# A mixture-of-experts layer behind sigmoid attention: the second expert product in row form, and the gathered rows turned by VectorE through DRAM

## The chip, the core and the metric

The kernel runs on one core of a Trainium2 chip. Its time is the device time of one execution in microseconds (us); lower is better. A core has five engines that work side by side, each on its own in-order list of instructions: TensorE (PE in the profile, with its weight loads shown apart as PEld), VectorE (DVE), ScalarE (ACT), GpSimd (POOL) and SyncE (SP, which here only issues DMAs). Matmul results go to PSUM, which has eight banks of 512 fp32 words per partition; a tile of two banks is called wide below.

## The reference: what is computed

```python
scores = scale * np.matmul(q, k.transpose(0, 1, 3, 2)) - np.log(S)   # 8 x 12 heads, 448 tokens, 64 dims
attn = 1.0 / (1.0 + np.exp(-scores))
x = np.matmul(attn, v)            # brought to 3584 tokens x 768
logits = x @ w_gate               # 3584 x 8
order = np.argsort(-logits.flatten())
for idx in order:                 # greedy: each expert takes at most 448 tokens
    tok, e = idx // 8, idx % 8
    if assigned[tok] < 0 and counts[e] < 448:
        assigned[tok] = e; counts[e] += 1
for e in range(8):                # x: 768 -> 1024 -> 768
    out[assigned == e] = np.maximum(x[assigned == e] @ w1[e], 0) @ w2[e]
```

Every expert ends with exactly 448 tokens.

## The kernel before, in words

**Attention (first 278 us or so).** For every pair of heads TensorE makes scores, ScalarE the sigmoid, TensorE the product with v. The result is kept turned, and `rows` writes it as rows of 768 to the DRAM tensor `xs`.

**Routing.** The greedy assignment is done expert by expert by the class `Router`. One phase finds the next expert that fills up, and the threshold that its 448th token has, by a search of 16 steps (`search`, L157 to L218), then makes the list of its tokens (`pick`, `place`, `lists`; the list is `idx`, L293). From the second phase on a search step is VectorE work alone: three counting passes (L173), two small block transposes (L189, L195), a sum and some scalar operations. TensorE takes part at the ends of a phase: L162 turns the keys, L224 turns the threshold `kap` that the search has found (VectorE L217), L252, L257, L258, L284 and L291 make the list. Phase 0 runs before the experts, phases 1 to 7 while the experts run.

**Experts.** `moe(kx)` (L660) makes the two products of one expert. Every fp32 operand is split into a high part and a rest (`wh`/`wl`, `xh`/`xl`, `hh`/`hl`), and a product is the sum of three matmuls (high-high, high-rest, rest-high). Both products hold the weights still (128 x 128) and move the 448 tokens: 144 matmuls of 448 columns for the first product (L680 to L684), 144 for the second (L715 to L719). Because of that the second product comes out turned, 768 features by 448 tokens; `untranspose` (L641) brings it back, in 12 pairs of TensorE transposes per expert (L645), each with a copy by ScalarE (L650), and then scatters the rows to `out` (L653). The weights come in pieces through SP's queue (`load_w`, L573) and are split by ScalarE (L596) and GpSimd (L598; for the last two experts every other one on VectorE).

**Rows of the next expert.** When the list of the next expert is there, `prepare` (L752) puts its work into `chores`: four gathers of 128 rows from `xs` (L618, GpSimd's queue), and eight `xturn` (L621), each three TensorE transposes (L632), a ScalarE copy (L635) and a VectorE subtraction (L636) that yield `xh` and `xl`, the turned input of the first product.

**What sets the order.** Nothing is scheduled at run time: the order of each engine's list is written by the loop at the end (L767 to L787). It walks through the matmuls of `moe`, adds an assumed price for each to `clock` (MM, 189 ns), and, when the clock passes a due time, puts in the next step of the router (due times from T_DVE and the like) or the next chore. So the search steps of phase k+1 stand in VectorE's list among the chores for the expert of phase k, and L224 stands in TensorE's list after as many matmuls as the assumed prices make of a search.

**PSUM.** `ps_t` has two single banks (transposes), `ps_s` two wide tiles (the products), `ps_a` two single banks (the router).

## Time and profile before

| | us |
|---|---|
| three runs, median | 890.27 (887.0, 890.27, 893.16) |
| the profiled execution, its own time | 887.23 |
| its span, from the first to the last instruction | 885.5 |
| first matmul of the experts (L680) | 335.31 |
| start of the last matmul of the experts (L719) | 877.14 |

| engine | busy, us | share of the span |
|---|---|---|
| PE | 837.8 | 95% |
| PEld | 639.0 | 72% |
| DVE | 531.4 | 60% |
| POOL | 467.4 | 53% |
| ACT | 456.2 | 52% |

How to read it: shares over the whole span mix the attention with the experts. For the experts, from 335 us on, the views that count are the busy time by stretch, the instructions in order of time on one engine (with the idle time ahead of each and who ended it), and the groups of instructions with their mean duration. A matmul's shown duration contains its way through the array and overlaps its neighbours, so its cost in a row of matmuls is the distance from one start to the next.

### The profile page before, as it was taken

Reading aid. Unit: us, or ns where it says so; the run is one execution under the profiler, and the core shown is the slowest. Engines: PE = TensorE matmul, PEld = TensorE weight load, DVE = VectorE, ACT = ScalarE, POOL = GpSimd, SP = SyncE. Lnnn points to the kernel's source line nnn. Section 1 sums busy time; section 2 is a strip of 40 time slices with the busy share of each in tenths; the row PEclk is TensorE's granted clock in tenths of the full one; section 3 lists DMA queues with packets and bytes.
Section 4 is the critical chain, followed back from the end, with each engine's and each line's share of the span. In section 5 each row is a group of like instructions: output and inputs, shape, how many; then the busy total and the mean of one; then the engine's idle time right before and its main releaser. Section 6 shows DMA issues by size and latency. Waiting matters only on the chain.

```text
span 885.5 us, 16232 instructions
## 1 busy us (share of the span) xinstructions
PE 837.8 (95%) x5507; PEld 639.0 (72%) x5507; DVE 531.4 (60%) x2047; ACT 456.2 (52%) x610; POOL 467.4 (53%) x449
## 2 busy tenths in 40 slices
PE   6999999999998729998999999999999999999996
PEld 3455455455555518987988988988888888889996
DVE  4665555555554778958869779779689521421110
ACT  6777777777774724434424424434434434443431
POOL 9645444444400014846864964873883882752651
PEclk9999999999999969999999999999999999999999
DMA  9876666665603945434443542452552542632511
GB/s 172 168 144 127 132 125 123 131 126 120 138 12 100 299 161 153 136 107 161 136 133 117 146 156 75 157 164 95 153 164 70 178 146 72 228 111 72 192 49 63
DMA packets 203507, 117.57 MB, mean 133 GB/s; under 512 B 143936, under 2 KB 193088, under 8 KB 203424
## 3 DMA queue, kind: packets, MB, share of 16 engines
q1 hardware_dynamic: 190688, 83.03, 36.0%
q0 software_dynamic: 10880, 33.28, 11.9%
q8 instruction: 43, 0.70, 0.3%
q10 hardware_dynamic: 1856, 0.23, 0.2%
q14 instruction: 40, 0.33, 0.1%
HBM read 94.47 MB, written 22.02 MB: 132 GB/s over the span
## 4 chain that ended last, share of the span: by engine, by line
PE 77%; DVE 8%; DMA 5%; issue 4%; POOL 3%; ACT 1%; SPq 1%; POOLq 0%; ACTq 0%; DVEq 0%
PE tp L461 13%; PE sc L437 11%; PE sc L682 8%; PE sc L680 8%; PE sc L684 8%; PE sc L717 6%; PE sc L719 6%; PE sc L715 6%; PE tp L467 2%; DMA xs<-xr 2%; DVE r_junk L173 2%; PE sc L447 2%; PE tp L645 2%; DMA xr<-xs,r_idx 2%; PE tp L632 2%
## 5 line engine op out<-in xcount | busy, mean ns | idle before, releaser
L598 POOL TENSOR_TENSOR wl<-wr,wh 128x768 fp32r<-128x768 f32 (+1 forms) x96 | 205.9, 2155 | 134.6 <-ACT wh L596 126.9
L427 ACT ACTIVATE at<-sc,bias 128x896 f32<-128x896 f32 x168 | 161.0, 1006 | 63.1 <-PE sc L447 38.2
L372 POOL DMA_DIRECT2D nkq<-in_q_dram x188 | 118.6, 646 | 111.5 <-DVE kqT L412 104.7
L719 PE MATMUL sc<-hh,wl 128*128 128x448 f32 (+2 forms) x400 | 151.4, 378 | 0.0
L717 PE MATMUL sc<-hl,wh 128*128 128x448 f32 (+2 forms) x400 | 145.4, 364 | 0.1
L684 PE MATMUL sc<-xh,wl 128*128 128x448 f32 (+2 forms) x396 | 145.4, 367 | 0.0
L682 PE MATMUL sc<-xl,wh 128*128 128x448 f32 (+2 forms) x396 | 144.9, 366 | 0.0
L715 PE MATMUL sc<-hh,wh 128*128 128x448 f32 (+2 forms) x400 | 143.9, 360 | 0.0
L680 PE MATMUL sc<-xh,wh 128*128 128x448 f32 (+2 forms) x396 | 143.8, 363 | 0.0
L173 DVE TENSOR_SCALAR_CACHE_REDUCE r_junk<-r_KE,r_T 128x224 bf16<-128x224 f32 x315 | 123.2, 441 | 0.1
L461 PE MATMUL tp<-at,nv 128*64 128x448 f32 x576 | 118.8, 548 | 0.0
L596 ACT ACTIVATE wh<-wr 128x768 fp32r<-128x768 f32 (+1 forms) x112 | 102.0, 939 | 13.2 <-DMA wr<-in_moe_w_dram 13.1
L692 POOL TENSOR_TENSOR hl<-yt,hh 128x896 fp32r<-128x896 f32 x32 | 68.3, 2136 | 44.5 <-ACT yt L691 41.8
L421 DVE TENSOR_TENSOR kqL<-kqT,kqH 128x896 fp32r<-128x896 f32 (+1 forms) x49 | 52.6, 1073 | 58.3 <-ACT kqH L419 58.2
L688 ACT ACTIVATE hh<-sc 128x896 fp32r<-128x896 f32 x32 | 29.5, 920 | 111.0 <-PE sc L684 111.0
L618 POOL DMA_INDIRECT xr<-xs,r_idx x32 | 32.0, 1002 | 97.5 <-ACT wh L596 86.7
L717 PEld LDWEIGHTS sc<-hl,wh 128*128 128x128 f32 x400 | 75.2, 188 | 7.0 <-issue 1.1
L598 DVE TENSOR_TENSOR wl<-wr,wh 128x768 fp32r<-128x768 f32 (+1 forms) x16 | 25.1, 1571 | 91.7 <-ACT wh L596 91.5
L461 PEld LDWEIGHTS tp<-at,nv 128*64 128x64 f32 x576 | 37.1, 136 | 59.1 <-issue 57.9
L682 PEld LDWEIGHTS sc<-xl,wh 128*128 128x128 f32 x396 | 74.5, 188 | 6.3 <-issue 0.5
L715 PEld LDWEIGHTS sc<-hh,wh 128*128 128x128 f32 x400 | 75.6, 189 | 4.4
L680 PEld LDWEIGHTS sc<-xh,wh 128*128 128x128 f32 x396 | 74.7, 189 | 5.5
(156 smaller groups left out, 1323.7 us busy)
## 6 DMA issues: line engine op xcount, KB each, us to landing
wr<-in_moe_w_dram SPq DMA_DIRECT2D x64, 384.0 KB
wr<-in_moe_w_dram SPq DMA_DIRECT2D x48, 512.0 KB
xs<-xr SPq DMA_DIRECT2D x32, 336.0 KB
nkq<-in_k_dram SPq DMA_DIRECT2D x190, 56.0 KB
nkq<-in_q_dram POOLq DMA_DIRECT2D x188, 56.0 KB, 2.6
nv<-in_v_dram SPq DMA_DIRECT2D x92, 96.0 KB
nr<-in_v_dram SPq DMA_DIRECT2D x46, 32.0 KB
xr<-xs,r_idx POOLq DMA_INDIRECT x32, 4.4
```

Source lines behind the costliest of these rows:

```text
L173: nc.vector.tensor_scalar(junk, KE, T[:, i:i + 1].bitcast(F32), None, OP.is_ge, OP.add, accum_out=cnt[:, i:i + 1])
L372: qn.dma_start(t[o:o + 32, n], rws[x])
L427: nc.scalar.activation(a, p[:, :, :S], AF.Sigmoid, bias=bias, scale=1 / math.sqrt(D))
L461: nc.tensor.matmul(p[j * 64:j * 64 + 64, :S], nat["v", b, g][:, h0 + j, c, :], AT[b, pr, c][:, j, :], start=(c == 0), stop=(c == 2 and pr ...
L596: nc.scalar.activation(hi, raw[u], AF.Copy)
L598: eng.tensor_tensor(lo, raw[u], hi.bitcast(F32), OP.subtract)
L680: nc.tensor.matmul(ph[:, f, lo:hi], wh[:, a, fs], xh[:, dd, lo:hi], start=st, stop=False)
L682: nc.tensor.matmul(ph[:, f, lo:hi], wh[:, a, fs], xl[:, dd, lo:hi], start=False, stop=False)
L684: nc.tensor.matmul(ph[:, f, lo:hi], wl[:, a, fs], xh[:, dd, lo:hi], start=False, stop=en)
L715: nc.tensor.matmul(py[:, d2, :w], wh[:, a, dsl], h1, start=st, stop=False)
L717: nc.tensor.matmul(py[:, d2, :w], wh[:, a, dsl], h2, start=False, stop=False)
L719: nc.tensor.matmul(py[:, d2, :w], wl[:, a, dsl], h1, start=False, stop=(j == 1 and a == 3))
```

## The change

It has four parts, and nothing in attention or in the routing itself changes.

1. **Second product in row form.** The hidden values are now held still, 128 tokens at a time, and 384 columns of `w2` move. The result comes out as rows of tokens and needs no turning back. 448 tokens are three blocks of 128 and one of 64; for the last one the high part and the rest of 64 tokens each share one block of 128 (`hr`), whose two halves are added afterwards (L748 to L753). Per expert 176 matmuls of 384 columns (L738) stand where 144 of 448 columns and 24 transposes stood. `w2` comes in eight pieces of 128 x 768, not six of 128 x 1024.
2. **Rows of the experts from the third on turned by VectorE.** `stage` writes the gathered rows to a DRAM buffer `xq` (SP's queue), `fetch` reads them back in four parts, so that 32 tokens by 192 features lie on each group of 32 partitions, and `vturn` turns them in blocks of 32 x 32 on VectorE (L641), copies on ScalarE (L643) and subtracts on VectorE (L644). Four `vturn` per expert stand where eight `xturn` stood. Feature 6p + a now stands on partition p, so `w1` is read in that order, and the remaining `xturn` (experts 0 and 1) take every sixth column.
3. **PSUM.** `ps_t` is gone, `ps_s` has three wide tiles, and `xturn` uses the router's banks.
4. **Prices and buffers.** MM2 = 164 ns for the 384-column matmuls, fewer row buffers, W_DVE moved so that it still names the last two experts.

The order of the instructions moves with it. VectorE, in the search of phase 4 before (the rows are those of expert 3; `xl` is the rest of the turned rows, `r_junk` the counting passes):

```order
L636 TENSOR_TENSOR xl<-tp,xh 128x3x128
L173 TENSOR_SCALAR r_junk,c_CN<-r_KE,r_T 128x224 x3
L189 STREAM_TRANSPOSE r_ct<-c_CN 128x32
L191 TENSOR_SCALAR rt<-c_kk,r_J 128x3
L193 TENSOR_REDUCE r_s_6891<-r_ct 128x2
L195 STREAM_TRANSPOSE r_ct<-r_s_6891 128x32
L197 TENSOR_SCALAR r_j_6887,r_acc<-r_ct 128x3
L210 SCALAR_TENSOR_TENSOR r_T<-r_acc,rt 128x3
L212 TENSOR_SCALAR r_J<-r_acc,r_J 128x1
L636 TENSOR_TENSOR xl<-tp,xh 128x3x128 x2
```

Now, in the search of phase 3 (the rows are those of expert 2):

```order
L641 STREAM_TRANSPOSE xt<-xw 128x256 x3
L644 TENSOR_TENSOR xl<-xt,xh 128x3x256
L173 TENSOR_SCALAR r_junk,c_CN<-r_KE,r_T 128x224 x3
L189 STREAM_TRANSPOSE r_ct<-c_CN 128x32
L191 TENSOR_SCALAR rt<-c_kk,r_J 128x3
L193 TENSOR_REDUCE r_s_6161<-r_ct 128x2
L195 STREAM_TRANSPOSE r_ct<-r_s_6161 128x32
L197 TENSOR_SCALAR r_j_6157,r_acc<-r_ct 128x3
L210 SCALAR_TENSOR_TENSOR r_T<-r_acc,rt 128x3
L212 TENSOR_SCALAR r_J<-r_acc,r_J 128x1
L641 STREAM_TRANSPOSE xt<-xw 128x256 x3
L644 TENSOR_TENSOR xl<-xt,xh 128x3x256
```

Where one subtraction stood between two search steps, three transposes and a subtraction of twice the width stand, with a ScalarE copy between them. There are four such groups per expert, and for the experts 2, 3, 4 and 5 they lie in the searches of phases 3, 4, 5 and 6; for the experts 6 and 7 they come after the last search.

TensorE, in a second product (`yt` is the turned result before; `hb` and `hr` are the hidden values now). Before:

```order
L645 MATMUL tp<-ident,yt 128x128 x2
L719 MATMUL sc<-hh,wl 128x448
L715 MATMUL sc<-hh,wh 128x448
L717 MATMUL sc<-hl,wh 128x448
L719 MATMUL sc<-hh,wl 128x448
```

Now, and no transpose stands among them:

```order
L738 MATMUL sc<-wh,hr 128x384
L738 MATMUL sc<-wl,hr 128x384
L738 MATMUL sc<-wh,hb 128x384 x2
L738 MATMUL sc<-wl,hb 128x384
L162 MATMUL rt<-ident,r_KT 128x112 x2
```

Counted over the whole list, 207, 212, 218 and 221 matmuls of the products stand between L162 and L224 in the phases 3 to 6 (74, 112, 152 and 176 of them of 384 columns, the others of 448); before it was 196 to 198 of 448 columns with 24 transposes of rows and 16 to 24 of results.

SP's queue, where the rows of expert 2 go to DRAM and back (`wr` are the weights); before, only the weights stood there:

```order
L584 DMA wr<-in_moe_w_dram 128x3x256
L623 DMA xq_3959<-xr 128x768 x2
L584 ISA
L584 DMA wr<-in_moe_w_dram 128x3x256
L623 DMA xq_3959<-xr 128x768
L630 DMA xw<-xq_3959 32x8x192 x4
L623 DMA xq_3959<-xr 64x768
L584 ISA
L584 DMA wr<-in_moe_w_dram 128x3x256
L630 DMA xw<-xq_3959 32x6x192 x4
```

The write to `xq` waits for the gather, the read back for the write, and the weights issued after them wait in the same queue.

The diff, cut to its core:

```diff
-        ps_t = ctx.enter_context(tc.tile_pool(name="ps_t", bufs=2, space=PSUM))
-        ps_s = ctx.enter_context(tc.tile_pool(name="ps_s", bufs=2, space=PSUM))
+        ps_s = ctx.enter_context(tc.tile_pool(name="ps_s", bufs=3, space=PSUM))
...
+        def stage(kx, j, n):
+            nc.sync.dma_start(xq[kx % 2][j * 128:j * 128 + n], xg[kx, j][:n])
+
+        def fetch(kx, j0, j1):
+            t = xg[kx, 4 + j0] = xp.tile([128, 8, DM // 4], F32, name="xw", bufs=2)
+            v = xq[kx % 2].rearrange("(j c) (i w) -> i c j w", c=32, i=4)
+            for i in range(4):
+                nc.sync.dma_start(t[32 * i:32 * i + 32, :j1 - j0], v[i, :, j0:j1])
+
+        def vturn(kx, j0, j1, hf):
...
+            w = xg[kx, 4 + j0].rearrange("p j (w a) -> p a j w", a=ND)
+            t = xp.tile([128, 3, 256], F32, name="xt", bufs=2)[:, :, :32 * n]
+            for a in range(3):
+                nc.vector.transpose(t[:, a].rearrange("p (j w) -> p j w", w=32), w[:, hf * 3 + a, :n])
+            sl = (slice(None), slice(hf * 3, hf * 3 + 3), slice(32 * j0, 32 * j1))
+            nc.scalar.activation(xh[sl], t, AF.Copy)
+            nc.vector.tensor_tensor(xl[sl], t, xh[sl].bitcast(F32), OP.subtract)
...
-                p = ps_t.tile([128, 512], F32, name="tp")
+                p = R.bank()
...
-                nc.tensor.transpose(p[:, i * n:(i + 1) * n], xg[kx, j][:n, dd * 128:(dd + 1) * 128], ident[:n, :n])
+                nc.tensor.transpose(p[:, i * n:(i + 1) * n], xg[kx, j][:n, dd::ND], ident[:n, :n])
...
+            for i in range(2):
+                cs = slice(i * W2, (i + 1) * W2)
+                py = [ps_s.tile([128, 2, 512], F32, name="sc") for _ in range(2)]
+                for j in range(4):
...
+                    for z in range(2):
+                        for a in range(2):
...
+                            for c in range(2):
+                                o = py[z][:, c, :W2]
+                                if z == 0 or c == 0:
+                                    t = slice((2 * z + c) * 128, (2 * z + c + 1) * 128)
+                                    terms = ((h[:, 0, t], wh), (h[:, 1, t], wh), (h[:, 0, t], wl))
+                                else:
+                                    terms = ((r, wh), (r, wl))
+                                for n, (hs, w) in enumerate(terms):
+                                    nc.tensor.matmul(o, hs, w[:, a], start=st and n == 0,
+                                                     stop=en and n == len(terms) - 1)
+                                    yield MM2
...
+                if kx:
+                    for j, n in blocks():
+                        chores.append((t0 + 1500 * j + 6000, kx + 1, lambda j=j, n=n: stage(kx + 1, j, n)))
+                        if j % 2:
+                            r = (4 * j - 4, min(4 * j + 4, S // 32))
+                            t = t0 + 1500 * j + 8500
+                            chores.append((t, kx + 1, lambda r=r: fetch(kx + 1, *r)))
+                            for hf in range(2):
+                                chores.append((t + 4500 + 1500 * hf, kx + 1,
+                                               lambda r=r, hf=hf: vturn(kx + 1, *r, hf)))
+                    chores.sort(key=lambda c: c[0])
+                    return
```

More of the change, by code (lines that the diff above doesn't have):

```diff
@@ L25 @@
 AT_BUFS = 8
-YT_BUFS = 3
+YR_BUFS = 3
 LATE_PER_STEP = 2
@@ L34 @@
 FIRST = 4000.0
-W_DVE = 84
+W_DVE = 96
 class Consts:
@@ L610, in moe_attention @@
         xg, XH = {}, {}
+        xq = [dr.tile([S, DM], F32, name=f"xq{i}") for i in range(2)]
         def blocks():
@@ L638, in moe_attention, with scatter @@
         scat, chores = [], []
-        MM = 189
-        def untranspose(kx, yr, i, yt, j, n, t0=0, end=False):
-            p = R.bank() if end and j % 2 else ps_t.tile([128, 512], F32, name="tp")
-            for d2 in range(2):
-                nc.tensor.transpose(p[:n, d2 * 128:(d2 + 1) * 128], yt[:, d2, j * 128 - t0:j * 128 - t0 + n], ident)
-            dst = yr[j][:n, i * 256:(i + 1) * 256]
-            if end and j % 2:
-                nc.vector.tensor_copy(dst, p[:n, :256])
-            else:
-                nc.scalar.copy(dst, p[:n, :256])
-            if i == 2:
-                nc.gpsimd.memset(spacer, 0.0)
-                ins = nc.gpsimd.indirect_dma_start(
-                    out=out, out_offset=bass.IndirectOffsetOnAxis(ap=listed[kx][:n, j:j + 1], axis=0),
-                    in_=yr[j][:n], in_offset=None)
-                for o in scat:
-                    tc.declare_no_dep(ins.ins, o.ins, reason="rows of other tokens")
-                scat.append(ins)
+        MM, MM2, W2 = 189, 164, 384
+        def scatter(kx, yr, j, n):
+            nc.gpsimd.memset(spacer, 0.0)
+            ins = nc.gpsimd.indirect_dma_start(
+                out=out, out_offset=bass.IndirectOffsetOnAxis(ap=listed[kx][:n, j:j + 1], axis=0),
+                in_=yr[j // 2][:n, j % 2], in_offset=None)
+            for o in scat:
+                tc.declare_no_dep(ins.ins, o.ins, reason="rows of other tokens")
+            scat.append(ins)
         def moe(kx):
@@ new lines, in moe @@
+                for h1, h2, t in parts:
+                    if kx < H_POOL:
+                        nc.gpsimd.tensor_tensor(h2, h0[:, :, t], h1.bitcast(F32), OP.subtract)
+                    else:
+                        nc.vector.scalar_tensor_tensor(h2, ph[:, :, t], 0.0, h1.bitcast(F32), OP.max, OP.subtract)
+                hb.append((h, r))
+            yr = [xp.tile([128, 2, DM], F32, name="yr", bufs=YR_BUFS) for _ in range(2)]
+            for i in range(2):
+                cs = slice(i * W2, (i + 1) * W2)
+                py = [ps_s.tile([128, 2, 512], F32, name="sc") for _ in range(2)]
+                for j in range(4):
+                    u = u0 + 8 + 4 * i + j
+                    state['u'] = max(state['u'], u)
+                    stream(state['u'])
+                    wh, wl = split[u]
+                    for z in range(2):
+                        for a in range(2):
+                            f = 2 * j + a
+                            h, r = hb[j][0][:, a], hb[j][1][:, a]
+                            st, en = f == 0, f == 7
+                            for c in range(2):
[3 more added lines that the diff above has]
+                                    terms = ((h[:, 0, t], wh), (h[:, 1, t], wh), (h[:, 0, t], wl))
+                                else:
+                                    terms = ((r, wh), (r, wl))
[3 more added lines that the diff above has]
+                                    yield MM2
+                        if j == 3:
+                            last = (kx, i) == (E - 1, 1)
+                            if z == 0:
+                                nc.scalar.copy(yr[0][:, :, cs], py[0][:, :, :W2])
+                            else:
+                                (nc.vector.tensor_copy if last else nc.scalar.copy)(yr[1][:, 0, cs], py[1][:, 0, :W2])
+                                e = hp.tile([64, W2], F32, name="rest", bufs=2)
+                                nc.scalar.copy(e, py[1][64:, 1, :W2])
+                                if last:
+                                    nc.vector.tensor_tensor(yr[1][:64, 1, cs], py[1][:64, 1, :W2], e, OP.add)
+                                else:
+                                    nc.scalar.copy(yr[1][:64, 1, cs], py[1][:64, 1, :W2])
+                                    nc.gpsimd.tensor_tensor(yr[1][:64, 1, cs], yr[1][:64, 1, cs], e, OP.add)
+                            if i == 1:
+                                for jj, n in blocks():
+                                    if jj // 2 == z:
+                                        chores.append((clock[0] + 1500 + 500 * (jj % 2), kx + 2,
+                                                       lambda jj=jj, n=n: scatter(kx, yr, jj, n)))
```

73 lines of the change are left out of this document (22 added, 51 removed).

## The prediction, made before the changed kernel ran

> **What bounds the kernel now.** I read the page first. Over the whole span PE is busy 95%, but that mixes attention, which is left as it is, with the experts. So the second view is the busy time by stretch (start and end, length, then busy time and count for PE, PEld, DVE, ACT and POOL, granted clock, DMA share, GB/s), for three stretches inside the experts:
>
> ```profile
> 454.00:516.00 62.00, 61.05 (x345) 53.54 (x343) 50.85 (x265) 26.16 (x41) 42.90 (x29) 1.00 0.45 141
> 516.00:579.00 63.00, 61.75 (x350) 54.01 (x349) 51.10 (x265) 28.01 (x45) 39.39 (x28) 1.00 0.42 132
> 579.00:641.00 62.00, 61.70 (x351) 54.11 (x350) 50.15 (x264) 26.34 (x42) 41.17 (x29) 1.00 0.43 136
> ```
>
> TensorE leaves 0.3 to 1.25 us of 62 idle: it sets the pace. But VectorE is second with 50 to 51 of 62, far ahead of ScalarE. A change that takes work from TensorE and gives it to VectorE is to be read against that 50, and against where in the list the work stands. So the third view is the instructions in order of time, over one phase of the router (start, duration, engine, line; in brackets the wait and who ended it):
>
> ```profile
> 586.42 0.38 PE L162 MATMUL rt<-ident,r_KT 112*128 112x112 f32 x2 [0.30 <-DVE r_KT L153]
> 586.84 0.39 DVE L165 COPY r_KE<-rt 128x224 f32<-128x224 f32 x1 [0.57 <-PE rt L162]
> ...
> 628.96 0.15 DVE L217 TENSOR_SCALAR r_kap<-r_J 128x1 int32<-128x1 int32 x1
> 632.30 0.27 PE L224 MATMUL rt<-ident,r_kap 128*112 128x128 f32 x1
> 632.61 0.17 DVE L227 TENSOR_REDUCE r_km<-rt 112x1 f32<-112x8 f32 x1 [3.50 <-PE rt L224]
> ```
>
> VectorE's search runs from 586.84 to 629.11, 42.3 us. TensorE reaches L224 45.9 us after L162, and VectorE then waits 3.50 us for it. That wait is the whole reserve: TensorE would stand still at L224 as soon as the search took about 3.5 us more, or TensorE's own work between the two lines took 3.5 us less. The change does both.
>
> **The change part by part: TensorE.** Its price in a row of matmuls is the distance between starts.
>
> ```profile
> 336.13 0.28 PE L680 MATMUL sc<-xh,wh 128*128 128x256 f32 x1
> 337.44 0.28 PE L684 MATMUL sc<-xh,wl 128*128 128x256 f32 x1
> 346.04 0.39 PE L680 MATMUL sc<-xh,wh 128*128 128x448 f32 x1
> 367.75 0.36 PE L684 MATMUL sc<-xh,wl 128*128 128x448 f32 x1
> ```
>
> The first two rows begin and end a run of 12 matmuls of 256 columns: 1.31/11 = 0.119 us. The other two begin and end 108 matmuls of 448 columns: 21.71/107 = 0.203 us. No matmul of 384 columns is in the trace; it lies between these bounds, and I take the straight line, 0.119 + 128/192 x 0.084 = 0.175 us. The second products cost 8 x 144 x 0.203 = 233.7 us and will cost 8 x 176 x 0.175 = 246.4: **+12.7**.
>
> What leaves TensorE is transposes:
>
> ```profile
> 394.13 0.37 PE L717 MATMUL sc<-hl,wh 128*128 128x448 f32 x1
> 394.33 0.38 PE L645 MATMUL tp<-ident,yt 128*128 128x128 f32 x2
> 394.76 0.37 PE L715 MATMUL sc<-hh,wh 128*128 128x448 f32 x1
> ...
> 729.78 0.36 PE L717 MATMUL sc<-hl,wh 128*128 128x448 f32 x1
> 729.98 0.49 PE L632 MATMUL tp<-ident,xr 128*128 128x128 f32 x3
> 730.51 0.36 PE L715 MATMUL sc<-hh,wh 128*128 128x448 f32 x1
> ```
>
> From L717 to L715 lie normally two matmuls, 0.406 us. With a pair of L645 between them it is 0.63, so a pair costs 0.224 us; 8 x 12 pairs: **-21.5**. With a triple of L632 it is 0.73, so 0.324; eight triples in each of six experts: **-15.6**. A few of these triples also waited for VectorE or for the gathered rows; I put **-2** for that by the group of waits
>
> ```profile
> PE tp L632 <- DVE xl L636: 3.2, 5, 0.9
> ```
>
> (sum, times, longest). On TensorE alone the change is worth 12.7 - 21.5 - 15.6 - 2 = **-26.4 us**.
>
> The Trainium skill ("TensorE: Matmul & The Clock Gate", section "Back-to-back issue gap") has a rule for one matmul behind another, columns/2.4 + 2.5 ns. It gives 162.5 ns for 384 columns, 12.5 less than my line, and by it the 890 or so matmuls that lie outside the stalls below would save another 11 us. But for 448 columns it gives 189 where the rows above have 203, so I stay with the line.
>
> **VectorE.** The subtraction of the turned rows leaves the search and the four `vturn` come in. What leaves:
>
> ```profile
> L636 DVE TENSOR_TENSOR xl<-tp,xh 128x384 fp32r<-128x384 f32 x45 | 23.8, 551 | 19.6 <-ACT xh L635 19.4
> L636 DVE TENSOR_TENSOR xl<-tp,xh 128x192 fp32r<-128x192 f32 x15 | 5.2, 352 | 5.0 <-ACT xh L635 4.8
> ```
>
> (busy time, mean ns, idle before). Six of the first and two of the second lie in each search: 4.0 us, which leaves 38.3 for the search itself. What comes has no row of its own; the nearest are
>
> ```profile
> L412 DVE STREAM_TRANSPOSE kqT<-nkq 128x896 f32<-128x896 f32 x47 | 51.9, 1104 | 4.0 <-DMA nv<-in_v_dram 2.5 <-DMA nkq<-in_k_dram 0.8 <-issue 0.2
> L189 DVE STREAM_TRANSPOSE r_ct<-c_CN 128x32 f32<-128x32 f32 x96 | 20.3, 212 | 3.3
> L421 DVE TENSOR_TENSOR kqL<-kqT,kqH 128x896 fp32r<-128x896 f32 x47 | 51.4, 1093 | 58.2 <-ACT kqH L419 58.2
> L598 DVE TENSOR_TENSOR wl<-wr,wh 128x768 fp32r<-128x768 f32 x10 | 15.3, 1541 | 52.7 <-ACT wh L596 52.5 <-issue 0.2
> L419 ACT ACTIVATE kqH<-kqT 128x896 fp32r<-128x896 f32 x47 | 44.5, 947 | 2.4 <-DVE kqT L412 2.2
> L596 ACT ACTIVATE wh<-wr 128x768 fp32r<-128x768 f32 x64 | 52.7, 847 | 13.2 <-DMA wr<-in_moe_w_dram 13.1
> ```
>
> Transposes: 212 to 1104 ns over 864 columns is 1.03 ns per column, so 443 ns for 256 columns and 377 for 192; two groups of three of each make 4.9 us per expert. They read with a stride of six words, which none of these rows does; the bound above is the ratio of a reduction that reads across its rows to an operation of the same size that doesn't,
>
> ```profile
> L146 DVE TENSOR_REDUCE rt<-ML 112x32 f32<-112x256 f32 x5 | 3.1, 610 | 0.2
> L147 DVE TENSOR_TENSOR rt<-ML,rt 112x256 f32<-112x256 f32 x5 | 2.1, 429 | 0.2
> ```
>
> 1.42, which would add 2.1 us; the bound below is that it costs nothing. The ScalarE copy: VectorE's next instruction is the subtraction that needs it, so VectorE stands still meanwhile. In L421 the same trip took 58.2/47 = 1.24 us, of which 0.95 was the copy (L419), so 0.29 beside it. With 847 ns (L596, 768 elements) a trip is 1.14, with three quarters of the elements some 0.98 (an estimate); four of them 4.2 us. The subtraction: in proportion to L421 0.94 and 0.70 us, after L598 1.54 and 1.16; four of them 3.3 to 5.4. Together **12.4 to 14.5 us per expert**, 16.6 with the stride. If ScalarE is just splitting a piece of weights, or a part of the rows is late, a little more. I take **14**.
>
> The Trainium skill ("SBUF — State Buffer", section "Who interferes with whom") speaks for the upper end: a VectorE instruction with both inputs in SBUF and a GpSimd instruction that reads SBUF exclude each other. L636 had one input in PSUM, L644 has both in SBUF, and GpSimd is subtracting weights for two thirds of these stretches. By the rule the price would be 14.5, by the lower row 12.4, and the sums below differ by 4 x 2.1 = 8 us; L598 beside L421 is the trace's sign that the rule holds.
>
> **Where it lies.** The order of VectorE shows the four groups of experts 2 to 5 between the search steps of phases 3 to 6. Behind each waiting subtraction stand all the later steps, behind these L217, and on TensorE L224 waits for L217 with all matmuls behind it. TensorE's work between L162 and L224 is now, in phase 3, 74 x 0.175 + 133 x 0.203 = 39.9 us; in the phases 4 to 6 (112 and 100, 152 and 66, 176 and 45 matmuls) 39.9, 40.0 and 39.9. With 0.3 for L162, 40.2. The search: 0.4 from L162 to L165, 38.3, 14, and 0.2 to L224, makes 52.9. TensorE stands still for 52.9 - 40.2 = 12.7 us, less some 0.2 of small waits inside its work: **12.5 us, four times: +50**. Nothing else fills that hole, since the next matmuls stand behind L224 in TensorE's own list. In phases 1 and 2 VectorE has no `vturn` in the search, and for experts 6 and 7 they come after the last one: there nothing is lost.
>
> **The clock.** Such a hole is long enough to lose the clock. At the start of the experts (same columns as above):
>
> ```profile
> 326.00:330.00 4.00, 0.32 (x6) 0.13 (x2) 3.22 (x8) 0.91 (x2) 1.97 (x2) 0.50 0.11 23
> 333.00:335.00 2.00, 1.50 (x7) 1.29 (x7) 1.30 (x3) 0.99 (x3) 0.00 (x0) 0.50 0.99 292
> 335.00:336.00 1.00, 0.97 (x6) 0.78 (x5) 0.74 (x2) 0.64 (x2) 0.00 (x0) 0.75 0.91 217
> ```
>
> After a stretch with TensorE 8% busy the clock is 0.50, and it stays there for 2 us of dense work and half of the next. That is about 2.5 to 3 us at half speed, so 1.5 us lost each time: **+6** for four holes (0 to 11).
>
> **The transfers.** The rows now go gather, `xq`, back. In the phase above:
>
> ```profile
> 581.71 0.16 DVE L293 TENSOR_SCALAR r_idx<-rt 128x4 int32<-128x4 f32 x1 [0.91 <-PE rt L291]
> 582.77 0.99 POOL L618 DMA_INDIRECT xr<-xs,r_idx  x1
> 588.89 0.90 POOL L618 DMA_INDIRECT xr<-xs,r_idx  x1 [0.30 <-issue]
> ```
>
> and of the lists of DMAs and of the chain of waits
>
> ```profile
> xr<-xs,r_idx POOLq DMA_INDIRECT x32, 4.4
> 290.65 3.61 DMA xs<-xr
> ```
>
> The first and the last of the four gathers are issued 1 and 7 us after the list. A gather takes 4.4 us to landing, a trip of rows through SP's queue 3.6 (the write to `xs`), and now there are two trips more: the rows are back between 594 and 601. VectorE comes to the first group, which needs half of them, five steps into the search (38.3/16 = 2.4 us each), near 600. So the cover is thin there; the groups of the later parts have 5 us and more of room. If it fails the wait adds to the same hole. Row writes, copies of results and the extra additions on GpSimd (64 x 384, twice per expert) lie beside TensorE's work, with ScalarE at 26 and GpSimd at 43 of 62; I count them at nothing.
>
> **Sum.** 12.7 - 21.5 - 15.6 - 2 + 50 + 6 = +29.6 on the profiled execution's 887.2, so 916.8. The median of the runs shown, 890.3, lies 3.0 above that execution: **920 us**. Its own range: below, 12.4 us per expert (holes of 10.9) and no loss of clock, 907; above, 16.6 us (holes of 15.1) and 11 us of clock, 936.
>
> **Rivals.**
> 1. *The hole doesn't open; only TensorE's saving counts.* That needs `vturn` to cost VectorE under 2 us per expert. For it: the saving of 26.4 is sure, and VectorE is idle 11 of 62 us. Against it: that idle time lies outside the search, mostly the 3.5 us at L224 and the making of the list. Time: 887.2 - 26.4 + 3.0 = **864**.
> 2. *Only half a hole.* The ScalarE trips cost nothing and the subtractions go at L421's price: 4.9 + 3.3 = 8.2 us, holes of 6.7, 27 in all, too short to lose the whole clock (2): 887.2 - 26.4 + 29 + 3 = **893**, no change that can be told. For it: ScalarE is free over half of the time. Against it: no instruction stands between transposes and subtraction in VectorE's list.
> 3. *The rows come late.* SP takes its DMAs in order, and the weights ahead of the row writes wait there for buffers that GpSimd frees:
>
> ```profile
> SPq L585 <- POOL wl L598: 177.7, 38, 8.3
> ```
>
> 4.7 us on average, 8.3 at most. If such waits stand ahead of write and read-back, VectorE waits 6 us more in each of the four searches, and from there on the transfers, not VectorE, set the hole: 920 + 24 = **944**.
>
> **How the numbers follow.** Forecast 0.62, rival 1 0.12, rival 2 0.14, rival 3 0.12. The runs of before lie 0.7% apart, so about 1% can be told from no change. Slower by over 1% is the forecast and rival 3: 0.74; within 1% rival 2: 0.14; faster rival 1: 0.12. The range from 886 to 945 leaves out rival 1 and the outer half of rival 3.
>
> **What would show it.** Right: in the time order, TensorE idle for 10 to 15 us ahead of L224, released by L217, in four phases; VectorE never waiting for L224 there; granted clock below 1.00 just after; distance of starts at L738 near 0.175; no L645. Wrong: VectorE still waiting at L224 in those phases (rival 1), L644 without idle time before it (rival 2), or long waits of L641 for the DMA into `xw` (rival 3). A pace of L738 well off 0.175 would break the first term: 0.01 us is 14 us on TensorE, some 9 of them outside the holes.

## The result, and the profile after

| | before | after |
|---|---|---|
| median of the runs, us | 890.05 | 955.84 |
| ratio, 95% interval | | 1.0743 (1.071 to 1.0776) |
| span of the profiled execution, us | 885.5 | 954.5 |
| mean granted clock | 0.984 | 0.942 |

The change costs 66 us. The direction was forecast, the size was not: +30 stood in the sum, and 945 was the upper end of the range.

Where the time went is read from the same view as before, the busy time by stretch. I cut it at two events that both kernels have, the list of expert 2 and the list of the next to last expert (L293 on VectorE). Before:

```profile
335.00:456.50 121.50, 118.16 (x692) 105.64 (x691) 97.33 (x516) 50.30 (x75) 77.71 (x46) 1.00 0.42 130
456.50:705.90 249.40, 246.45 (x1391) 215.65 (x1391) 201.98 (x1057) 105.23 (x167) 166.07 (x113) 1.00 0.43 135
705.90:878.30 172.40, 171.42 (x957) 154.88 (x958) 37.46 (x51) 72.56 (x113) 88.53 (x59) 1.00 0.36 119
```

After:

```profile
335.00:466.40 131.40, 122.44 (x700) 112.64 (x699) 99.89 (x517) 46.28 (x75) 78.71 (x58) 0.93 0.38 116
466.40:757.50 291.10, 236.78 (x1295) 217.17 (x1296) 234.88 (x1089) 98.27 (x148) 175.54 (x139) 0.91 0.49 152
757.50:946.00 188.50, 174.25 (x921) 163.51 (x921) 46.03 (x68) 66.29 (x99) 98.44 (x79) 0.95 0.45 141
```

The columns are start and end, length, then busy time of PE, PEld, DVE, ACT and POOL, and the clock. The three stretches grew by 9.9, 41.7 and 16.1 us. Call them the beginning (experts 0 and 1, no row is turned by VectorE), the middle (the phases 3 to 6, four searches with `vturn` in them) and the end (the last two experts, no search any more). In the middle TensorE is idle for 54 us where it was idle for 3, and VectorE is busy 33 us more.

One phase of the middle on VectorE, as the prediction asked for it (time, duration, in brackets the wait):

```profile
547.57 0.39 DVE L165 COPY r_KE<-rt 128x224 f32<-128x224 f32 x1 [0.57 <-PE rt L162]
...
561.06 1.71 DVE L641 STREAM_TRANSPOSE xt<-xw 128x256 f32<-128x256 f32 x3 [0.57 <-DMA xw<-xq]
563.68 0.96 DVE L644 TENSOR_TENSOR xl<-xt,xh 128x768 fp32r<-128x768 f32 x1 [0.91 <-ACT xh L643]
566.89 1.64 DVE L641 STREAM_TRANSPOSE xt<-xw 128x256 f32<-128x256 f32 x3
569.44 0.96 DVE L644 TENSOR_TENSOR xl<-xt,xh 128x768 fp32r<-128x768 f32 x1 [0.91 <-ACT xh L643]
...
599.14 0.15 DVE L217 TENSOR_SCALAR r_kap<-r_J 128x1 int32<-128x1 int32 x1
```

The search lasts 51.7 us; it was 42.3. The turning of one expert costs VectorE about 12.7 us: 6.0 of transposes, 3.3 of waiting for ScalarE's copy, 3.4 of subtraction. That is inside the 12.4 to 14.5 of the prediction.

But the holes on TensorE do not stand where they were expected:

```profile
501.06 0.74 PE L696 MATMUL sc<-xh,wh 128*128 128x448 f32 x1 [16.80 <-ACT xh L643]
572.38 0.74 PE L696 MATMUL sc<-xh,wh 128*128 128x448 f32 x1 [5.40 <-ACT xh L643]
599.35 0.32 PE L224 MATMUL rt<-ident,r_kap 128*112 128x128 f32 x1 [1.85 <-DVE r_kap L217]
643.39 1.01 PE L738 MATMUL sc<-wh,hb 128*128 128x384 f32 x2 [4.97 <-ACT wh L595]
669.63 0.46 PE L224 MATMUL rt<-ident,r_kap 128*112 128x128 f32 x1 [5.21 <-DVE r_kap L217]
722.50 1.01 PE L738 MATMUL sc<-wh,hb 128*128 128x384 f32 x2 [14.21 <-ACT yr L744]
```

Only 7 us of them stand at L224. TensorE waits for the rows of the next expert (22 us), for a copy of results by ScalarE (14) and for split weights (5). So there are two questions: does VectorE set the time of the middle, as predicted, or ScalarE, whose queue is the releaser in four of these six rows? And where do the 26 us at the two ends come from?

### The profile page after: what moved, and what is told of

The parts are those of the page before. It is cut to its first block, busy times and chain, and to the rows that moved or that the text cites. A ratio compares the mean times of both kernels' runs of the same rounds, so it can differ in the third digit from the quotient of the medians.

```text
span 954.5 us, 16204 instructions
## 1 busy us (share of the span) xinstructions
PE 834.1 (87%) x5379; PEld 654.9 (69%) x5379; DVE 576.0 (60%) x2097; ACT 438.7 (46%) x577; POOL 489.6 (51%) x510
## 5 line engine op out<-in xcount | busy, mean ns | idle before, releaser
L597 POOL TENSOR_TENSOR wl<-wr,wh 128x768 fp32r<-128x768 f32 x110 | 204.6, 1874 | 74.1 <-ACT wh L595 73.9
L738 PE MATMUL sc<-wh,hb 128*128 128x384 f32 x768 | 204.1, 346 | 22.8 <-ACT yr L744 14.2
L738 PEld LDWEIGHTS sc<-wh,hb 128*128 128x128 f32 x768 | 143.4, 195 | 25.3 <-ACT yr L744 14.5
L698 PE MATMUL sc<-xl,wh 128*128 128x448 f32 (+2 forms) x396 | 148.5, 375 | 0.1
L595 ACT ACTIVATE wh<-wr 128x768 fp32r<-128x768 f32 x128 | 103.6, 848 | 77.4 <-PE sc L738 38.4
L738 PE MATMUL sc<-wl,hb 128*128 128x384 f32 x384 | 132.7, 345 | 6.0 <-POOL wl L597 5.9
L706 ACT ACTIVATE hb<-sc 128x768 fp32r<-128x768 f32 x32 | 26.0, 813 | 147.5 <-PE sc L700 147.5
L712 POOL TENSOR_TENSOR hb<-h,hb 128x768 fp32r<-128x768 f32 x32 | 59.9, 1872 | 65.2 <-ACT h L709 65.1
L700 PEld LDWEIGHTS sc<-xh,wl 128*128 128x128 f32 x396 | 77.6, 196 | 11.3 <-POOL wl L597 4.0
L597 DVE TENSOR_TENSOR wl<-wr,wh 128x768 fp32r<-128x768 f32 x18 | 23.6, 1313 | 96.1 <-ACT wh L595 95.9
L738 PEld LDWEIGHTS sc<-wl,hb 128*128 128x128 f32 x384 | 74.5, 194 | 7.9 <-POOL wl L597 7.8
```

The costliest lines, as they stand in the source:

```text
L595: nc.scalar.activation(hi, raw[u], AF.Copy)
L597: eng.tensor_tensor(lo, raw[u], hi.bitcast(F32), OP.subtract)
L698: nc.tensor.matmul(ph[:, f, lo:hi], wh[:, a, fs], xl[:, dd, lo:hi], start=False, stop=False)
L700: nc.tensor.matmul(ph[:, f, lo:hi], wl[:, a, fs], xh[:, dd, lo:hi], start=False, stop=en)
L712: nc.gpsimd.tensor_tensor(h2, h0[:, :, t], h1.bitcast(F32), OP.subtract)
L738: nc.tensor.matmul(o, hs, w[:, a], start=st and n == 0, stop=en and n == len(terms) - 1)
```

## The experiments

All ratios are against runs of the kernel before on the same chip. The lengths of the three stretches (from 335 us on, in us) come from the rows of L293 and the last matmul of each run; the first matmul of the experts comes at 335.3 us before, at 336.1 in the change and at 333.6 to 335.8 in the others, so the beginnings compare only to 1 or 2 us; where it matters they are counted from that matmul. Stretches made by the same instructions differ by as much: so counted, the beginning is 128.6 to 130.4 us in the eight runs that are the change up to there (the change, A, B, D, E, G, H, I), and the middle is 291.1 in the change and 293.5 in I.

| run | median, us | ratio (95% interval) | beginning | middle | end |
|---|---|---|---|---|---|
| before | 890.05 | 1 | 121.5 | 249.4 | 172.4 |
| the change | 955.84 | 1.0743 (1.071 to 1.0776) | 131.4 | 291.1 | 188.5 |
| A copy by VectorE | 960.56 | 1.0796 (1.0762 to 1.083) | 129.0 | 307.3 | 178.7 |
| B no turning from expert 2 on | 876.96 | 0.9859 (0.9831 to 0.9888) | 128.9 | 233.9 | 168.5 |
| C turning part alone | 956.08 | 1.0753 (1.0725 to 1.0782) | 124.2 | 291.0 | 195.7 |
| D transposes twice | 987.48 | 1.1079 (1.103 to 1.1127) | 130.3 | 313.2 | 201.3 |
| E no write to `xq` | 938.05 | 1.0528 (1.0484 to 1.0571) | 127.6 | 287.5 | 177.4 |
| F search steps later | 1059.1 | 1.1907 (1.1877 to 1.1938) | 148.5 | 398.3 | 166.9 |
| G holes filled | 954.48 | 1.0718 (1.0686 to 1.075) | 129.7 | 293.8 | 188.0 |
| H holes filled to the end | 955.37 | 1.0723 (1.0705 to 1.074) | 128.1 | 291.7 | 189.9 |
| I last turns later | 951.04 | 1.0672 (1.0649 to 1.0695) | 130.5 | 293.5 | 183.4 |
| J banks of its own | 956.40 | 1.0737 (1.0715 to 1.0758) | 124.9 | 296.6 | 189.9 |
| K TensorE turns all | 918.49 | 1.0328 (1.0298 to 1.0359) | 130.9 | 266.3 | 176.0 |
| L row form, contiguous | 914.14 | 1.0268 (1.0226 to 1.031) | 127.0 | 266.9 | 174.6 |
| M row form, banks of its own | 892.20 | 1.0022 (1.0002 to 1.0042) | 121.7 | 247.6 | 174.7 |
| N M with due times moved | 887.43 | 0.9968 (0.9953 to 0.9982) | 124.7 | 249.9 | 166.2 |

### A: is it ScalarE's queue?

```diff
-            nc.scalar.activation(xh[sl], t, AF.Copy)
+            nc.vector.tensor_copy(xh[sl], t)
```

> Edit: the copy to xh in vturn (L643) is done by VectorE, between its transposes and its subtraction; ScalarE has no part in the turning. Theory Q (ScalarE's queue): L643 stands at the head of ScalarE's queue until VectorE has turned (84 us in 24 waits), and the weight splits and result copies behind it come late; TensorE's waits for wh (13 us), wl (8 us) and the result copy L744 (14 us) go, with their clock loss, some 40 us: about 915. Theory S (the search is too long, as predicted): VectorE's price per expert goes only from 13.1 to about 12 us, and a hole that closes at one place opens at L224 instead: about 945 to 950, with longer waits of L224 for L217 in phases 5 and 6.

The run is slower, not 40 us faster, so in the middle ScalarE's queue is not the cause. As S said, most holes with ScalarE as the releaser closed (one of 7 us for a result copy is left) and others opened at L224. The instructions of TensorE in order of time:

```profile
573.60 0.71 PE L696 MATMUL sc<-xh,wh 128*128 128x448 f32 x1 [8.54 <-DVE xh L643]
600.90 0.46 PE L224 MATMUL rt<-ident,r_kap 128*112 128x128 f32 x1 [4.41 <-DVE r_kap L217]
675.55 0.46 PE L224 MATMUL rt<-ident,r_kap 128*112 128x128 f32 x1 [10.85 <-DVE r_kap L217]
757.78 0.46 PE L224 MATMUL rt<-ident,r_kap 128*112 128x128 f32 x1 [12.66 <-DVE r_kap L217]
```

The lesson for reading: the releaser named in a wait is the last link only. ScalarE's copy L643 was itself waiting for VectorE. The 960.6 itself lies above both forecasts: that the middle got 16 us longer was expected by neither theory; 4.8 us of it are shown under the last heading, and the rest stays open. The end got 10 us shorter: there Q has something.

### B: how much hangs on the turning?

```diff
-                        chores.append((t0 + 1500 * j + 6000, kx + 1, lambda j=j, n=n: stage(kx + 1, j, n)))
-                        if j % 2:
...
+                        XH[kx + 1] = XH[1]
```

> Edit: stage, fetch and vturn are left out, and the experts from the third on use the turned rows of the second (so their results are for other rows); gathers, routing, TensorE's order and all else stay. S and Q: TensorE's saving of 25 us is left, less the waits and clock loss of phases 1 and 2, which do not come from vturn (about 5 idle and 7 of clock): about 875, TensorE without holes over 2 us after 420. P: holes stay at the weights and result copies, over 900.

877, as S and Q expected. The middle is 233.9 us, 57 less than with the turning and 15.5 less than before. In the stretch of the middle (same columns) TensorE is nearly full again, with the same matmuls in the same order; one hole over 2 us is left, 4.0 us ahead of L224 in phase 3, where no such hole was expected:

```profile
463.90:697.80 233.90, 226.41 (x1295) 209.77 (x1296) 197.93 (x1025) 86.98 (x132) 175.16 (x139) 0.99 0.45 142
```

So row form, smaller pieces of weights and PSUM split do not make these holes. The end is 168.5 us, 20 less than in the change and 3.9 less than before: there the turning costs 20 us. What this run does not do is the turning by anyone, so 877 is no version to have.

### C and D: the turning alone, and twice

C puts part 2 into the kernel before and leaves its second product as it was. Beside the functions of part 2:

```diff
-XR_BUFS = 12
+XR_BUFS = 10
...
-                src = w1[ds(gate[kx], 1)].rearrange("e (a p) f -> p (e a) f", p=128)
+                src = w1[ds(gate[kx], 1)].rearrange("e (p a) f -> p (e a) f", a=ND)
```

> Edit: the kernel before with part 2 alone (rows of the experts from the third on through xq and vturn, w1 read in the other order), second product as before, ten row buffers instead of twelve. S: TensorE has 43.4 us of work between L162 and L224 against a search of 52, so holes of 9 us in four phases, -15.6 of transposes, 2.5 us of clock per hole, and the late rows of the last two experts: 890 + 35 to 45. Q: ScalarE is held as in the changed kernel and has more to do here (copies of the turned results), so the result copies and splits come late as well: 890 + 55 or more. If the row form were the cause of the loss: about 875.

It took 956, all of the loss without the row form: 67 us more than before. The middle is as long as in the change (291.0), although TensorE has more work in it. That is the mark of a stretch that another engine sets. S, which had 35 to 45, missed by over 20: the end is 23 us longer than before, and the late rows there had no number in it. The figure agrees with the 55 or more of Q, yet by A ScalarE's queue can't be the reason for the middle.

```diff
-            for a in range(3):
+            for a in (0, 1, 2, 0, 1, 2):
                 nc.vector.transpose(t[:, a]...
```

> Edit: each of the transposes in vturn is done twice into the same tile; nothing else. It adds 5.7 us of VectorE per expert. S: each of the four phases gets longer by just that, 23 us, and the last two experts by 0 to 11: 978 to 990. If VectorE's time were covered (T), less than 8 us: below 964.

The transposes of the whole run, six experts, now take

```profile
L641 DVE STREAM_TRANSPOSE xt<-xw 128x256 f32<-128x256 f32 (+1 forms) x144 | 69.2, 544 | 30.9 <-DMA xw<-xq 30.9
```

where 72 of them took 36.1 us, so 5.5 us more per expert. The middle grows by 22.1 us for 4 times 5.5: one for one. The end grows by 12.8 for 2 times 5.5. VectorE's time is on the path without cover in the middle, and at the end as well.

### E and I: the end

E leaves out the write to `xq` and reads rows that are there from the start, so other rows are turned.

```diff
-                        chores.append((t0 + 1500 * j + 6000, kx + 1, lambda j=j, n=n: stage(kx + 1, j, n)))
...
-            v = xq[kx % 2].rearrange("(j c) (i w) -> i c j w", c=32, i=4)
+            v = xs[:S].rearrange("(j c) (i w) -> i c j w", c=32, i=4)
```

> Edit: the rows are not written to xq; the read-back takes the first 448 rows of xs instead, which are there from the start (so other rows are turned; gathers, turning and all else stay). Theory S (VectorE's time in the phases): the 53 us of holes in phases 3 to 6 stay, since VectorE waits for the read-back only 0.6, 0.3 and 4.9 us there: 945 or more. Theory T (transfers): the waits of L641 (30 us), of SP's queue for the gathers (100 us) and the late weights behind them go; the last two experts lose no 16 us of holes and 5 of clock, and phase 6 gains 5: about 930.

The answer lies between the two: the middle loses 4 us, the end 11. Of the 20 us that the turning costs at the end by B, 11 go with the write and the waits for it; in the middle it is 4 of 57. In the change VectorE waits at the end for the rows, and ScalarE for VectorE, with a split of weights behind it for which TensorE waits. VectorE's rows:

```profile
780.16 1.73 DVE L641 STREAM_TRANSPOSE xt<-xw 128x256 f32<-128x256 f32 x3 [11.16 <-DMA xw<-xq]
834.98 1.76 DVE L641 STREAM_TRANSPOSE xt<-xw 128x256 f32<-128x256 f32 x3 [13.36 <-DMA xw<-xq]
```

ScalarE's:

```profile
836.78 0.84 ACT L643 ACTIVATE xh<-xt 128x768 fp32r<-128x768 f32 x1 [6.97 <-DVE xt L641]
...
840.95 0.83 ACT L595 ACTIVATE wh<-wr 128x768 fp32r<-128x768 f32 x1
```

TensorE's:

```profile
841.82 0.74 PE L696 MATMUL sc<-xh,wh 128*128 128x448 f32 x1 [4.44 <-ACT wh L595]
```

The chain is read upwards: matmul, split L595, behind L643 in ScalarE's queue, transposes L641, read-back. I takes only the held queue away, by asking for these turns 9 us later:

```diff
+                            t += 9000 if kx + 1 >= 6 else 0
                             for hf in range(2):
                                 chores.append((t + 4500 + 1500 * hf, kx + 1,
```

> Edit: the changed kernel with the four vturn of the experts 6 and 7 due 9 us of assumed time later; everything else, TensorE's order too, stays. After the last list TensorE needs 188.5 us against 172.4 before. Theory H (held queue): VectorE waits there 11 and 13 us for the read-back, L643 waits for VectorE at the head of ScalarE's queue, and the weight splits behind it are what TensorE waits for; 9 us later the rows have come, nothing is held, and the 8 us of waits for wh and some of the 6 for wl go: 942 to 948, the stretch after the last list 176 to 181. Theory T (late transfers): SP's queue waits for the gathers and the weights themselves come late, whenever VectorE turns: 953 or more.

951: the end is 183.4, 5 us shorter, less than Theory H and more than Theory T expected. For expert 6 VectorE still waits 10 us for the read-back, so the queue was not fully freed. Held queue and late transfers both have a part, and by D so has VectorE's own time; these parts overlap, and how the 20 us divide among them stays open.

### F: would more room in the order help?

```diff
-T_KEYS, ..., T_DVE, ... = 3600, 2100, 2050, 2025, ...
+T_KEYS, ..., T_DVE, ... = 3600, 2100, 2050, 2800, ...
```

> Edit: the changed kernel with a search step priced at 2800 ns of assumed time instead of 2025, so that 12 us more of TensorE's work stand between L162 and L224 and between one search step and the next. S: VectorE has the same work in series in phases 3 to 6, and the lists only come later against TensorE's work; what was waited for at L224 or behind ScalarE is waited for at the first matmul of the next expert: 945 to 975. Theory O (the fixed order is at fault, a search that TensorE's list gives room would cover the turning): 925 or less.

1059, against both. I had left out that the list of the next expert now comes when TensorE has no matmul left at all. The turning has gone out of the searches of the phases 3 to 6, which take 38.6 to 40.2 us, and stands ahead of them, where TensorE waits for it. TensorE's rows:

```profile
483.25 0.22 PE L291 MATMUL rt<-c_SEL,r_bt 128*64 128x4 f16 x2 [0.33 <-DVE r_bt L287]
513.39 0.74 PE L696 MATMUL sc<-xh,wh 128*128 128x448 f32 x1 [29.92 <-ACT xh L643]
```

From the end of the list to the first matmul with its rows it takes 30 us through DRAM and VectorE, here with nothing beside it. So at this price what the order gives to the search it takes from the way of the rows; prices between 2025 and 2800 were not tried.

### G and H: what the lost clock costs

Useless transposes of the identity stand where TensorE waits, into a bank of the router that is free.

```diff
+        def busy(n):
+            p = R.bank()
+            for _ in range(n):
+                nc.tensor.transpose(p[:, :128], ident, ident)
...
+            if kx in (2, 3):
+                busy(130 if kx == 2 else 28)
...
+                    if (kx, i, j) == (3, 1, 3):
+                        busy(28)
                     for z in range(2):
+                        if (kx, i, j, z) == (4, 1, 0, 1):
+                            busy(105)
```

> Edit: the changed kernel with useless transposes of the identity into a free router bank where TensorE stands still: 130 before the first product of expert 2 (a hole of 17 us), 28 before that of expert 3 (5 us) and 28 and 105 in the second products of experts 3 and 4 (5 and 14 us), at 0.108 us each so that they end 2 to 3 us before the hole does. Theory C (the clock): after each hole TensorE loses 2 to 2.5 us at half clock, so the useless work saves about 9 us: 944 to 949. If the lower clock costs no time (TensorE waits for VectorE anyway): 953 to 958.

954.5, but this run tells nothing about the clock: 2.2 to 3.4 us of waiting were left at the end of the holes, and just behind the two long ones the clock was 0.57 and 0.61. H has more of them, 148, 46, 40 and 127 in place of 130, 28, 28 and 105.

> Edit: as the run with useless transposes in four holes, but with more of them (148, 46, 40 and 127 instead of 130, 28, 28 and 105), since there TensorE still waited 2.8, 3.0, 2.2 and 3.4 us at the end and the granted clock just after was 0.57 and 0.61: the clock was lost all the same. Now less than 1 us is left. Theory C: the clock stays up and each of the four holes saves 2 us: 945 to 949. If VectorE sets the pace of these phases and a slower TensorE only shortens its next hole: 953 to 957, with the clock near 1 after the holes.

Now 0.6 to 1.2 us are left, and the clock stays behind the two long holes (behind experts' rows at 498 and result copy at 722). H:

```profile
499.60:503.60 4.00, 4.00 (x22) 3.62 (x20) 3.11 (x15) 2.15 (x3) 1.93 (x3) 1.00 0.00 0
723.50:727.50 4.00, 4.00 (x25) 4.00 (x24) 3.75 (x27) 2.12 (x3) 4.00 (x3) 1.00 0.02 3
```

The change at the same places:

```profile
501.00:505.00 4.00, 3.89 (x9) 3.13 (x10) 3.21 (x8) 1.92 (x4) 0.42 (x1) 0.50 0.00 0
722.50:726.50 4.00, 4.00 (x12) 4.00 (x13) 3.79 (x25) 3.42 (x6) 2.62 (x2) 0.50 0.00 0
```

Behind the two short holes it still fell, to 0.58 and 0.59. Over the whole middle the clock is 0.97 where it was 0.91. And the time is the same, 955.4, with the middle at 291.7. TensorE does twice as much behind a long hole (22 and 25 matmuls for 9 and 12) and waits longer at the next one (6.4 us, the useless work counted in, for 5.4). The clock is lost in the change, but in the middle that costs nothing. The end was not tried.

### J to N: the beginning, and the row form by itself

K undoes part 2 for all experts.

```diff
-                if kx:
+                if kx >= E:
                     for j, n in blocks():
                         chores.append((t0 + 1500 * j + 6000, ...
```

> Edit: part 2 undone for all experts: eight xturn per expert by TensorE, no write to xq and back; the row form of the second product, the new PSUM split and the prices stay. Both S and Q put nearly all of the loss on the turning by VectorE: 890 + 12.7 (384 columns) - 21.5 (no turning back) = 881, plus the wait of xturn for the router's two banks, which was 5.8 us for expert 1 in the changed kernel where before had 3: up to 6 x 3 us more and some clock, 881 to 905. A theory P, by which the row form or the three wide tiles themselves cost (later copies, weights in smaller pieces), says over 920.

918 is above my 881 to 905, though P, which asked for over 920, is not met either. Two edits that the list of the change names and the sum did not price are in it. L takes away one, the strided columns, with the order in which `w1` is read:

```diff
-                src = w1[ds(gate[kx], 1)].rearrange("e (p a) f -> p (e a) f", a=ND)
+                src = w1[ds(gate[kx], 1)].rearrange("e (a p) f -> p (e a) f", p=128)
...
-                nc.tensor.transpose(p[:, i * n:(i + 1) * n], xg[kx, j][:n, dd::ND], ident[:n, :n])
+                nc.tensor.transpose(p[:, i * n:(i + 1) * n], xg[kx, j][:n, dd * 128:(dd + 1) * 128], ident[:n, :n])
```

> Edit: the row form, three wide tiles and prices of the changed kernel; the rows of every expert turned by TensorE from contiguous columns, w1 read as before (so no strided reads). Against the run with strided columns (918.5) it takes away what the stride costs TensorE: its busy time was 8.5 us above the sum there, so about 910 if the rest is the wait for the router's two banks (theory B: 23 us of idle time, 7 of clock); about 880 if the waits came from the stride as well.

It is 914: the stride costs about 4 us here (the two intervals just overlap). In the groups by line the transposes L657 of K and of L are, one fence each:

```profile
L657 PE MATMUL rt<-ident,xr 128*128 128x128 f32 x135 | 28.8, 325 | 23.7 <-DVE xl L661 18.1 <-DVE r_w L149 5.2 <-DMA xr<-xs,r_idx 0.4
```

```profile
L657 PE MATMUL rt<-ident,xr 128*128 128x128 f32 x135 | 25.8, 304 | 24.7 <-DVE xl L661 18.8 <-DVE r_w L149 5.3 <-DMA xr<-xs,r_idx 0.4
```

M takes away the other, the shared banks:

```diff
+        ps_t = ctx.enter_context(tc.tile_pool(name="ps_t", bufs=2, space=PSUM))
-        ps_s = ctx.enter_context(tc.tile_pool(name="ps_s", bufs=3, space=PSUM))
+        ps_s = ctx.enter_context(tc.tile_pool(name="ps_s", bufs=2, space=PSUM))
...
-                p = R.bank()
+                p = ps_t.tile([128, 512], F32, name="tp")
```

> Edit: as the run before, but with two single banks for xturn again and two wide tiles for the products. B: the waits for the router's banks go (-30 against the shared banks), but a half of the second product now waits for the copy of the half before, 15 times about 1 us: 880 + 15 = 895 or less, below the kernel with shared banks. If the shared banks cost nothing, it is slower than that one by about 15.

892, 22 us less, with one wide tile less in the same edit. By the groups of waits, TensorE waited for VectorE's subtraction 24.5 us in L and 7.9 us in M:

```profile
PE rt L657 <- DVE xl L661: 24.5, 19, 2.8
```

```profile
PE tp L658 <- DVE xl L662: 7.9, 7, 2.0
```

The waits for copies that I had expected of two wide tiles did not come. J puts the same banks into the change:

> Edit: the changed kernel with two single banks for xturn (experts 0 and 1) and two wide tiles for the products. By the time of the third list (466.4 in the changed kernel, 456.5 before) 10 us are lost ahead of any vturn. Theory B (banks): about half of it comes from sharing the router's banks (the row form alone lost 5.4 more by that list with shared banks than with its own), the other half from the strided columns, so the third list comes near 461 and the run at 949 to 952. If the row form itself or its prices are the cause: no change, 954 or more.

The list of expert 2 comes at 459.9 in place of 466.4. Counted from the first matmul of the experts, the beginning is 124.7 us in J, 130.3 in the change and 121.2 before, so Theory B is right for 5.6 of 9.1 us (4 to 6 by the spread of equal beginnings). The forecast of 949 to 952 failed all the same: the whole gains nothing, since the middle is longer by 5.5. There TensorE waits 11.5 us for a result copy ahead of expert 3; whether that comes from having two wide tiles was not tried. N moves due times of M:

```diff
-T_KEYS, ..., T_OH, T_BT = 3600, ..., 3800, 600
+T_KEYS, ..., T_OH, T_BT = 3600, ..., 5200, 600
...
-                        chores.append((t0 + lag + 1500 * j, kx + 1,
+                        chores.append((t0 + lag + 2100 * j, kx + 1,
```

> Edit: the row form with TensorE's turning in its own banks (892.2), with two due times moved: the xturn come two per 2100 ns of assumed time instead of two per 1500, and the one-hot step of the router is priced at 5200 ns instead of 3800. If the 8 us in which xturn waited for VectorE's subtraction and the 4 us of L284 come only from these due times, 881 to 886, which would be below both kernels; if the transposes wait wherever they stand, 892.

887.4, between the two forecasts, so the due times make some of these waits and not all. It is 0.3% below the kernel before, with an interval that just leaves out 1. It is the one version with right results that is below both kernels, by almost nothing: the row form itself is worth what it takes away less what it adds, as computed (-8.8 by the prediction's terms; M's TensorE was busy 528.0 us up to its last matmul, before 536.0), and the turning is what the change loses by.

## Why the prediction was wrong, point by point

**Right: the mechanism and size of the middle.** The sum had 50 us of holes for the four searches and 6 for the clock; of the saving of 26.4 us, the 17.6 for the rows' transposes and their waits belong to the experts 2 to 5 (the middle) and 6 and 7 (the end); if the other 8.8 are spread evenly over the experts' time, 15.8 fall into the middle, 2 into the beginning and 9 into the end. That makes +40 for the middle, and measured are +41.7. VectorE's price (14 taken, 12.7 measured), TensorE's own saving (without any turning, in B, the middle is 15.5 us shorter than before) and the pace of L738 all held. For the pace, two rows of the changed kernel that are six pieces of weights, 132 matmuls, apart:

```profile
923.09 0.33 PE L738 MATMUL sc<-wl,hr 128*128 128x384 f32 x1
...
945.97 0.34 PE L738 MATMUL sc<-wl,hr 128*128 128x384 f32 x1
```

22.88/132 is 0.173 us, with 0.175 taken. The idle time of TensorE in the middle rose by 51 us. B and D show that it is VectorE's time in series; A takes ScalarE's queue out of the turning and E the write to `xq`, and the middle gets longer by the one and only 4 us shorter by the other.

**Wrong in that part: the place, and the clock.** "TensorE stands still ... at L224" holds for 7 of the 51 us. The same lateness reaches TensorE by three ways, and which one bites first depends on where the list has a matmul that needs something. And the term **+6** is nothing, as H shows. What took its place in the middle is the search being longer than computed, by 9 us in all: 56.5, 51.7, 53.7 and 56.0 us against 52.3, with one VectorE instruction 5.6 us longer than its norm beside GpSimd (below) in the first and 4.9 us of waiting for the read-back in the last. That the two nearly cancel is luck.

**Wrong: "there nothing is lost".** This sentence on phases 1 and 2 and on the experts 6 and 7 is the step that failed; it carries nearly the whole miss. By the sum the beginning should have gained 2 us; it lost 9.9 (9.1 from the first matmul on). The change list named the router's banks for `xturn` and the strided columns, and neither had a price in the sum. J shows 5.6 us for the banks (with the third wide tile, which goes in the same edit). For the stride, counted in the same way, C, which has it and banks of its own, is 3.7 us above before, K 3.1 above L, and J 2.4 above M. So the two are most of the loss. For the end the sum had -9; it is +16.1. By B the turning costs 20 of these 25 us, and the other 5 stay open. "They come after the last one" looked only at the search. The row that I should have followed is ScalarE's: L643 waits in its queue for VectorE, VectorE for a read-back, and the weights stand behind both, in ScalarE's queue and in SP's. E and I show 11 and 5 us for these, and D shows that VectorE's own time is on this path too.

**The rivals.** Rival 3, late rows, came true at the end, and not in the middle, where I had put it: there the waits for the read-back were 0.6, 0.3 and 4.9 us. Rivals 1 and 2 are out: B has the time of rival 1 plus 13 only because nobody turns. By the upper row that the rule of the Trainium skill spoke for ("SBUF — State Buffer", section "Who interferes with whom") a subtraction of 768 elements was to take 1.54 us; in the phase above it took 0.96, and over the twelve of the run 1.01 on average, with 1.61 at worst. So here the lower row was right but for one, and the longest delays fell on other instructions. The rule of the Trainium skill ("TensorE: Matmul & The Clock Gate", section "Back-to-back issue gap") gave 162.5 ns for 384 columns; 173 were measured.

## What to carry to other kernels

Before work is moved to the second busiest engine, add up that engine's chain between two hand-overs, not its busy share: 42 us of 46 left 3.5, and the four searches grew by 9 to 14 us each. For every edit in the list, buffers and access patterns too, there must be a price in the sum, and for every new wait the instructions behind it on its own queue. And a wait's releaser is only its last link: test it by taking that link away before believing it.

## What the runs showed of the hardware

One VectorE instruction can last as long as several GpSimd instructions in a row that run beside it. L206 stands once in every phase. In the change it took 0.23 to 0.28 us in the four phases in which no GpSimd subtraction ran beside it, and 1.41 and 1.75 in phases 1 and 5, where it ended with the one subtraction that was running. In phase 3 it took 5.84, VectorE:

```profile
474.64 5.84 DVE L206 TENSOR_SCALAR r_T<-c_kk,r_J 128x3 int32<-128x3 int32 x1
```

and GpSimd at that time:

```profile
474.99 5.46 POOL L597 TENSOR_TENSOR wl<-wr,wh 128x768 fp32r<-128x768 f32 x3
```

These are three subtractions, and both rows end at 480.5. In A the copy of 576 elements, 0.56 us in the quickest four of the middle's eight, took 5.34 beside three such subtractions, which is 4.8 of the 7.0 us by which A's last phase, from list to list, is longer than the change's:

```profile
725.53 5.34 DVE L643 CAST xh<-xt 128x576 fp32r<-128x576 f32 x1
```

```profile
725.06 5.41 POOL L597 TENSOR_TENSOR wl<-wr,wh 128x768 fp32r<-128x768 f32 x3
```

The Trainium skill ("SBUF — State Buffer", section "Who interferes with whom") counts copies, casts and tensor_scalar among the VectorE instructions that can take the pair of ports shared with GpSimd, where the one that issues first keeps the other out for a whole instruction; here it was three in a row. In phase 1 a second subtraction followed at once, and L206 ended with the first all the same. That it is these ports was not tried.
